# A spectral two-head kernel on one core: B's odd input lent to C as a seventh block, C's comparison ordered by table, A's result stored in half rows

## The chip, the cores and the metric

The kernel runs on one core of one Trainium2 chip. The core has a matrix engine (PE, with its weight loads listed apart as PEld), three engines for element work (DVE, ACT and POOL), a queue engine that mainly issues transfers (SP), and 16 DMA engines that all queues share. The metric is the device time of one execution in microseconds (us); less is better. SBUF is the on-chip memory with 128 partitions, PSUM the place where matrix products land, HBM the chip's main memory, where inputs and outputs lie.

## The reference

Two heads are computed from separate inputs and joined along the last axis. A is a global filter: a real 2-D Fourier transform, a product with a complex weight, and the inverse transform. B is a Fourier mixing layer whose transform matrices are given as inputs; for the values that are given they are the cosine and sine tables of the two lengths.

```python
def _A_ref(x, w_r, w_i):
    B, S, D = x.shape                                  # 1, 2048, 512
    X = jnp.fft.rfft2(x, axes=(-2, -1)) * (w_r + 1j * w_i)
    return jnp.fft.irfft2(X, s=(S, D), axes=(-2, -1))

def _B_ref(x, dft_seq_re, dft_seq_im, dft_hid_re, dft_hid_im):
    a = jnp.einsum("bsd,ed->bse", x, dft_hid_re)
    b = jnp.einsum("bsd,ed->bse", x, dft_hid_im)
    return (jnp.einsum("ts,bse->bte", dft_seq_re, a)
            - jnp.einsum("ts,bse->bte", dft_seq_im, b))

return jnp.concatenate([a, b], axis=-1)
```

## The kernel before

The kernel has three strands of work that share the engines.

**A** (`a_work`, line 628) is a fast transform written as matrix products. `forward` loads A's input in eight pieces, folds it on DVE and transforms it. Eight slots `e` (`slot`, line 512) then each multiply by the weights `wa`, which POOL's queue loads into `w`, one slot after the other; POOL writes two columns of `w` (line 519), ACT changes the sign of one part (line 520), DVE does the products, PE transforms in and out, and ACT writes the slot's result to `zv` (line 592). `inverse` (line 595) needs all slots. It runs eight steps of 8 products each out of `zv` (ACT copies at line 611) and 16 steps out of the tile `sda`, eight for each half `c` of the hidden places (ACT copies at line 622 into `ob`, which lies in the region of `zv`). When a half `c` is done, two stores of 1 MB each bring it to `out_a` (line 626).

**B** (`b_work`) computes the layer with a fast transform as well. Its folded input lies in two tiles, the even one `ye` and the odd one `yo` (25 x 128 values a partition); nine products `b_hidden` read them for the last time, and eight `b_rows` write the result, half by a store from SP and half by an indirect store from POOL.

**C** checks that the matrices given are the tables that B's fast transform assumes. It reads all of `cm` (32 blocks of 1 MB, each in two loads of 512 KB from SP, line 332) and compares each with a table `tt` on DVE (`count`, line 317), which counts differences in `stat`. There are four tables `pr`, each loaded once (line 327, 1 MB, two buffers). A table serves four blocks (`tb` 0 to 3) of its first half, then DVE changes the sign of every other column (line 340), and it serves four blocks of its second half. The tables go in pairs: first halves of tables 0 and 1, second halves of 0 and 1, then 2 and 3. After 16 blocks, `compare_hidden` (line 347) does the same for the two hidden matrices: ACT writes the expected table into a block `t` (lines 352 to 355, four operations), SP loads `wd` into another (line 357), and DVE compares. In this text the blocks of `cm` are called cm0 to cm31 in the order in which C takes them, and the hidden pair t0, wd0, t1, wd1.

All of C's blocks, and B's four blocks of raw input, come out of one ring of six buffers (`XR`, `block`, line 304): a load into a buffer waits until DVE, or for B's blocks PE, is done with what lay there.

At the end DVE sums `stat`, PE adds over the partitions (line 717), DVE makes a flag (line 718), and every engine reads the flag and branches (lines 720 and 721): where a difference was found, B is computed from the matrices as they are (`_b_from_c`); with the values given that part is skipped.

The order in which each engine takes its work is the program's order, which a scheduler makes of the three strands. `B_AT` and `C_AT` give the step of A after which a piece of B or C is due; `pin` holds a comparison behind a given DVE instruction of A. SP takes its transfers strictly in turn, and so do ACT, DVE and POOL.

Of the kernel before, what the change touches and what calls it, by code (L numbers as in the profile page):

```python
# [10 lines left out]
F32 = mybir.dt.float32  # L11
# [5 lines left out]
P = 128  # L17

YB = 2
XR = 6  # L20


B_AT = [0, 5, 7, 7, 8, 9, 9, 9, 9, 11, 13, 13, 13, 13, 13, 18, 20, 20, 21, 23, 27, 31, 31, 32, 50, 50, 50]
# [3 lines left out]
TINY = 2.0**-111  # L27
# [180 lines left out]
def kernel(  # L208
# [19 lines left out]
    nc = tc.nc  # L228
    ADD, SUB, MUL = ALU.add, ALU.subtract, ALU.mult
# [17 lines left out]
    bp = first.enter_context(tc.tile_pool(name="bp", bufs=1))  # L247
# [4 lines left out]
    def region(name):  # L252

        return ap.tile([P, 8192], F32, name=name)
# [6 lines left out]
    def part(v, kb, *shape):  # L261

        v = v[:, 256 * kb : 256 * kb + math.prod(shape)]
        if len(shape) == 1:
            return v
        names = "abcde"[: len(shape)]
        return v.rearrange("p (%s) -> p %s" % (" ".join(names), " ".join(names)), **dict(zip(names, shape)))
# [8 lines left out]
    yo = bp.tile([P, 25, 128], F32, name="yo")  # L276
# [3 lines left out]
    odd = bp.tile([P, 2], F32, name="odd")  # L280
# [18 lines left out]
    def late(dst, src):  # L299

        with tc.issue_after(turned[-1].ins):
            nc.gpsimd.dma_start(dst, src)  # L302

    def block():
        return bp.tile([P, 4, 512], F32, name="xr", bufs=XR)

    hts = []
    pin = [None]
# [3 lines left out]
    def count(raw, v, scale, op=ALU.not_equal):  # L312

        i = used[0]
        used[0] += 1
        with tc.issue_after(pin[0].ins) if pin[0] is not None else ExitStack():
            nc.vector.scalar_tensor_tensor(raw, raw, scale, v, op0=MUL, op1=op, accum_out=stat[:, i : i + 1])  # L317

    def compare():

        for pair in ((0, 1), (2, 3)):
            ts = []
            for half in range(2):
                for k, pr in enumerate(pair):
                    if half == 0:
                        ts.append(bp.tile([P, 4, 513], F32, name="tt", bufs=2))
                        nc.sync.dma_start(ts[k], tabs["tt"][pr])
                    t = ts[k]
                    for tb in range(4):
                        raw = block()  # L330
                        for m in range(2):
                            nc.sync.dma_start(raw[:, 2 * m : 2 * m + 2], cm[m, tb, pr + 4 * half])  # L332
                        v = t[:, :, 512:0:-1] if tb % 2 else t[:, :, :512]
                        for m in (slice(0, 2), slice(2, 4)) if tb % 2 else (slice(0, 4),):
                            k = int(tb % 2 and m.start == 2)
                            count(raw[:, m], v[:, m], odd[:, k : k + 1] if tb in (1, 2) else -TINY if k else TINY)
                        yield 2.4
                    if half == 0:
                        with tc.issue_after(pin[0].ins) if pin[0] is not None else ExitStack():
                            nc.vector.tensor_scalar(t[:, :, 1::2], t[:, :, 1::2], -1.0, None, op0=MUL)  # L340

    def hidden_table():

# [3 lines left out]
    def compare_hidden():  # L347

        hidden_table()
        for m in range(2):  # L350
            t = block()
            nc.scalar.mul(t[:, :2, :257], ht[:, :, m], TINY)
            nc.scalar.mul(t[:, :2, 257:], ht[:, :, m, 255:0:-1], -TINY if m else TINY)
            for k in range(2):
                nc.scalar.mul(t[:, 2:, k::2], t[:, :2, k::2], -1.0 if k else 1.0)
            raw = block()
            nc.sync.dma_start(raw, wd[m])
            count(raw, t, TINY)
            yield 2.4
# [87 lines left out]
    def mm(*args, **kw):  # L447
        mma[0] = nc.tensor.matmul(*args, **kw)  # L448
# [146 lines left out]
    def inverse(zv):  # L595

        v = bp.tile([P, 2304], F32, name="ye")
        di = v[:, :1024].rearrange("p (h q n) -> p h q n", h=2, q=2)
        g16 = v[:, 1024:1280].rearrange("p (s n) -> p s n", s=2)
        nc.sync.dma_start(di, tabs["di"].rearrange("p (h q n) -> p h q n", h=2, q=2))  # L600
        nc.sync.dma_start(g16, tabs["g16"].rearrange("p (s n) -> p s n", s=2))
        gz = zv.rearrange("p s f -> p (s f)")
        u = part(region("sda"), 0, 16, 512)
        for g in range(0, 16, 2):
            pu = ps_a.tile([P, 2, 512], F32, name="pa")
            for k in range(2):
                for h in range(2):
                    for q in range(2):
                        mm(pu[:, k, 256 * h : 256 * h + 256], gz[:, 32 * h + 16 * q + g + k :: 64], di[:, h, q],
                           start=q == 0, stop=q == 1)  # L610
            nc.scalar.copy(u[:, g : g + 2], pu)  # L611
            yield
        both = g16[:, :1].to_broadcast([P, 2, 128])
        ob = part(region("zv"), 0, 2, 2, 2, 8, 128)
        for c in range(2):
            for g in range(0, 16, 2):
                po = ps_a.tile([P, 2, 2, 128], F32, name="pa")
                for k in range(2):
                    for h in range(2):
                        at = 256 * h + 128 * c  # L620
                        mm(po[:, k], u[:, g + k, at : at + 128], g16 if h else both, start=h == 0, stop=h == 1)
                nc.scalar.copy(ob[:, c, :, :, g // 2], po.rearrange("p k r s -> p r k s"))  # L622
                yield
            for r in range(2):
                at = 256 * r + 128 * c
                nc.sync.dma_start(out_a[at : at + 128], ob[:, c, r].rearrange("p x i m -> p (x i m)"))

    def a_work():
        zv = part(region("zv"), 0, 16, 512)
        yield from forward(zv)  # L630
        TT(out=we[:, :, :, 0], in0=wsp_sb[:, :, :, 0, 0], in1=wsp_sb[:, :, :, 1, 0], op=ADD)
        TT(out=we[:, :, :, 1], in0=wsp_sb[:, :, :, 0, 1], in1=wsp_sb[:, :, :, 1, 1], op=SUB)
        TT(out=we[:, 1:, 1, 1], in0=wsp_sb[:, 1:, 1, 1, 1], in1=wsp_sb[:, 1:, 1, 0, 1], op=SUB)
        for i, v in enumerate((1.0, -1.0, 1.0, -1.0, -1.0)):
            nc.vector.memset(signs[:, i : i + 1], v)
        mid = region("sda")
        gens = [slot(e, zv, mid) for e in range(8)]

        def stage(e):
            if 0 <= e < 8:  # L640
                next(gens[e], None)

        stage(0)
        stage(0)
        stage(1)
        yield 0.1
        for e in range(9):
            stage(e)
            if e < 8:
                yield 5.0  # L650
            stage(e + 1)
            stage(e + 2)
            yield 0.1
            stage(e - 1)
            yield 0.1
        yield from inverse(zv)

    def b_work():
        x = {0: b_load(0)}
        yield  # L660
        x.update({q: b_load(q) for q in range(1, 4)})
        nc.gpsimd.dma_start(fb, tabs["fb"])
        yield
        for q in range(4):
            ev = b_fold(x[q])
            yield
            for g in range(4 * q, 4 * q + 4):
                b_along(g, x[q], ev)
            if q == 0:
                nc.sync.dma_start(hc, tabs["hc"])  # L670
                nc.sync.dma_start(slots, tabs["slot"])
                hidden_table()
                nc.sync.dma_start(mb, tabs["mb"])
            yield
        z = short()
        zb = [part(z, 2 * k, 512) for k in range(9)]
        for e in range(9):
            b_hidden(e, zb)
            yield
        for o in range(8):  # L680
            b_rows(o, zb)
            yield

    def all_compared():
        c = compare()
        for _ in range(16):
            yield next(c)
        yield from compare_hidden()
        yield from c

    count(same[:, 0:1], same[:, 1:2], TINY, ALU.is_equal)
    a, b, c = a_work(), b_work(), all_compared()
# [5 lines left out]
    for n in range(100):  # L698
        if next(a, a) is a and not b_at:
            break  # L700
        while b_at and b_at[0] <= n:
            b_at.pop(0)
            k = len(B_AT) - len(b_at) - 1
# [135 lines left out]
```

## Time and profile before

| | before |
|---|---|
| median of 3 runs | 221.36 us (221.28 to 221.91) |
| the profiled execution, whole | 220.61 us |
| its span in the trace | 218.6 us |
| PE busy / DVE busy / ACT busy / POOL busy | 88% / 73% / 35% / 18% |
| mean granted PE clock | 0.929 |
| bytes moved by DMA | 69.68 MB, mean 319 GB/s |

The span runs from the first to the last instruction of the program; what lies around it in the profiled execution is 220.61 - 218.6 = 2.0 us. Times in views of the trace count from the span's start. Busy shares are averages over stages that wait for different things, so the stages are read one by one. In a row of a timeline stand start, duration, engine, line and operation, written tile <- tiles read; SPq marks a transfer's issue by SP, not the transfer.

### The profile page before, as it was taken

Reading aid. Unit: us, or ns where it says so; the run is one execution under the profiler, and the core shown is the slowest. Engines: PE = TensorE matmul, PEld = TensorE weight load, DVE = VectorE, ACT = ScalarE, POOL = GpSimd, SP = SyncE. Lnnn points to the kernel's source line nnn. Section 1 sums busy time; section 2 is a strip of 40 time slices with the busy share of each in tenths; the row PEclk is TensorE's granted clock in tenths of the full one; section 3 lists DMA queues with packets and bytes.
Section 4 is the critical chain, followed back from the end, with each engine's and each line's share of the span. In section 5 each row is a group of like instructions: output and inputs, shape, how many; then the busy total and the mean of one; then the engine's idle time right before and its main releaser. Section 6 shows DMA issues by size and latency. Waiting matters only on the chain. (4 is left out here: it accounts for less than half of the span.)

```text
span 218.6 us, 2541 instructions
## 1 busy us (share of the span) xinstructions
PE 192.2 (88%) x833; PEld 150.0 (69%) x833; DVE 158.9 (73%) x257; ACT 77.2 (35%) x159; POOL 39.2 (18%) x56
## 2 busy tenths in 40 slices
PE   7799999979959999999999967668999999999700
PEld 2687778858749576586866544466999998888600
DVE  1589400088684899999889979799994799989350
ACT  2034333083452224422416535447333133333300
POOL 4002220032270010232113443160050000000000
PEclk9999999999995699999999996767999999999985
DMA  6999999999999999972353274057899999999990
GB/s 215 389 408 387 379 401 403 404 408 390 381 387 384 385 408 406 391 231 89 116 194 105 97 280 178 16 189 288 338 418 411 416 408 407 410 411 420 388 393 13
DMA packets 20883, 69.68 MB, mean 319 GB/s; under 512 B 3616, under 2 KB 4000, under 8 KB 19456
## 3 DMA queue, kind: packets, MB, share of 16 engines
q1 hardware_dynamic: 16176, 58.05, 67.6%
q0 software_dynamic: 4400, 10.81, 14.1%
q10 hardware_dynamic: 288, 0.59, 0.7%
q8 instruction: 8, 0.13, 0.2%
q14 instruction: 11, 0.09, 0.1%
HBM read 56.85 MB, written 8.39 MB: 298 GB/s over the span
## 5 line engine op out<-in xcount | busy, mean ns | idle before, releaser
L317 DVE SCALAR_TENSOR_TENSOR xr<-xr,tt 128x1024 f32<-128x1024 f32 (+1 forms) x24 | 37.3, 1578 | 27.9 <-DMA xr<-in_cm 27.8
L317 DVE SCALAR_TENSOR_TENSOR xr<-xr,odd,tt 128x1024 f32<-128x1024 f32 (+1 forms) x24 | 38.7, 1637 | 6.0 <-DMA xr<-in_cm 6.0
L448 PE MATMUL pa<-ye,zv 128*128 128x256 f32 x128 | 30.3, 401 | 2.0 <-ACT zv L592 2.0
L448 PE MATMUL pa<-zb,sda 128*128 128x256 f32 x128 | 30.6, 395 | 1.4 <-DVE sda L233 1.4
L448 PEld LDWEIGHTS pa<-ye,zv 128*128 128x128 f32 x128 | 29.2, 306 | 3.0 <-ACT zv L592 2.3
L448 PEld LDWEIGHTS pa<-zb,sda 128*128 128x128 f32 x128 | 25.2, 199 | 8.6 <-DVE sda L233 2.3
L233 DVE TENSOR_TENSOR sda<-zv 128x512 f32<-128x512 f32 (+1 forms) x24 | 19.0, 821 | 12.8 <-DMA zv<-in_xa 7.2
L448 PE MATMUL pa<-ye,sda 128*128 128x256 f32 x128 | 27.8, 379 | 0.0
L448 PEld LDWEIGHTS pa<-ye,sda 128*128 128x128 f32 x128 | 24.3, 190 | 3.3
L448 PEld LDWEIGHTS pa<-slots,sda 128*128 128x128 f32 x128 | 19.6, 225 | 8.5 <-DVE sda L233 3.7
L448 PE MATMUL pa<-slots,sda 128*128 128x128 f32 (+1 forms) x128 | 21.2, 328 | 2.6 <-DVE sda L233 2.6
L233 DVE TENSOR_TENSOR sda<-sda 128x512 f32<-128x512 f32 (+1 forms) x34 | 22.9, 716 | 0.0
L492 POOL DMA_DIRECT2D zv<-zb x16 | 10.0, 631 | 48.7 <-ACT zb L488 32.9
L233 DVE TENSOR_TENSOR sda<-pa,sda 128x1024 f32<-128x1024 f32 (+1 forms) x16 | 17.8, 1152 | 0.5
L481 ACT COPY zb<-pa 128x1024 f32<-128x1024 f32 x8 | 8.1, 1012 | 25.8 <-PE pa L448 25.8
L432 POOL DMA_INDIRECT out_b<-yb,turn x8 | 12.4, 1554 | 25.0 <-ACT yb L422 23.9
L448 PE MATMUL pa<-zb 128*128 128x512 f32 x32 | 15.1, 598 | 1.2 <-ACT zb L481 1.2
L388 PE MATMUL pb<-fb,xr 128*128 128x128 f32 (+1 forms) x64 | 15.4, 327 | 0.5 <-DVE xr L233 0.5
L622 ACT COPY zv<-pa 128x512 f32<-128x512 f32 x16 | 9.4, 587 | 17.8 <-PE pa L448 17.8
L302 POOL DMA_DIRECT2D sda<-in_wa x16 | 11.4, 717 | 23.0 <-ACT zb L405 10.1
L388 PE MATMUL pb<-fb,yb 128*128 128x72 f32 x64 | 13.3, 295 | 2.4 <-DVE yb L233 1.4
L611 ACT COPY sda<-pa 128x1024 f32<-128x1024 f32 x8 | 8.1, 1016 | 19.2 <-PE pa L448 19.2
(83 smaller groups left out, 216.0 us busy)
## 6 DMA issues: line engine op xcount, KB each, us to landing
xr<-in_cm SPq DMA_DIRECT2D x64, 512.0 KB, 10.3
tt<-tab_tt SPq DMA_DIRECT2D x4, 1026.0 KB, 12.6
zv<-in_xa SPq DMA_DIRECT2D x8, 512.0 KB, 9.7
xr<-in_xb SPq DMA_DIRECT2D x16, 256.0 KB, 6.9
zv<-zb POOLq DMA_DIRECT2D x16, 256.0 KB, 8.4
sda<-in_wa POOLq DMA_DIRECT2D x16, 256.0 KB, 3.7
out_a<-zv SPq DMA_DIRECT2D x4, 1024.0 KB, 10.8
xr<-in_wd SPq DMA_DIRECT2D x2, 1024.0 KB
```

What stands on the lines that cost most here:

```text
L233: last[0] = nc.vector.tensor_tensor(**kw)
L302: nc.gpsimd.dma_start(dst, src)
L317: nc.vector.scalar_tensor_tensor(raw, raw, scale, v, op0=MUL, op1=op, accum_out=stat[:, i : i + 1])
L388: nc.tensor.matmul(bank[:, at : at + hi - lo], v[:, cols], f[:, lo:hi], start=True, stop=True)
L432: stores.append(nc.gpsimd.indirect_dma_start(out=out_b, out_offset=bass.IndirectOffsetOnAxis(ap=turn[:, o : o + 1], axis=0), in_=y[:, 1], ...
L448: mma[0] = nc.tensor.matmul(*args, **kw)
L481: nc.scalar.copy(zs[p], pd[p])
L492: turned.append(nc.gpsimd.dma_start(zv[at : at + 29 : 4], ys[:, k]))
L611: nc.scalar.copy(u[:, g : g + 2], pu)
L622: nc.scalar.copy(ob[:, c, :, :, g // 2], po.rearrange("p k r s -> p r k s"))
```

## The change

Three things are changed.

`block()` counts its calls. From the 21st on (`LENT` = 20) every seventh comes from the place of `yo` instead of the ring: the calls are four for B's input, 16 for cm0 to cm15, then t0, wd0, t1, wd1, cm16 and so on, so that t0, cm19 and cm26 lie in `yo`'s place.

`compare()` takes one table at a time: four blocks, the change of sign, four blocks, then the next table. Table 0 is thus done after cm7 and table 1 after cm15, instead of after cm11 and cm15.

A's result is stored after four steps of each half `c` as well as after eight, as 512 KB in pieces of 2 KB (four `i` by 128 values) instead of 1 MB in pieces of 8 KB.

```diff
+LENT = 20
...
+    blocks = [0]
+
     def block():
+
+        i = blocks[0] - LENT
+        blocks[0] += 1
+        if i >= 0 and i % (XR + 1) == 0:
+            more = bp.tile([P, 25, 128], F32, name="yo").rearrange("p s j -> p (s j)")
+            return more[:, :2048].rearrange("p (k d) -> p k d", k=4)
         return bp.tile([P, 4, 512], F32, name="xr", bufs=XR)
...
-        for pair in ((0, 1), (2, 3)):
-            ts = []
+        for pr in range(4):
+            t = bp.tile([P, 4, 513], F32, name="tt", bufs=2)
+            nc.sync.dma_start(t, tabs["tt"][pr])
             for half in range(2):
-                for k, pr in enumerate(pair):
-                    if half == 0:
-                        ts.append(bp.tile([P, 4, 513], F32, name="tt", bufs=2))
-                        nc.sync.dma_start(ts[k], tabs["tt"][pr])
-                    t = ts[k]
-                    for tb in range(4):
...
+                if half:
+                    with tc.issue_after(pin[0].ins) if pin[0] is not None else ExitStack():
+                        nc.vector.tensor_scalar(t[:, :, 1::2], t[:, :, 1::2], -1.0, None, op0=MUL)
+                for tb in range(4):
+                    raw = block()
...
+        rows = out_a.rearrange("d (x i m) -> d x i m", x=2, i=8)
         for c in range(2):
             for g in range(0, 16, 2):
...
                 nc.scalar.copy(ob[:, c, :, :, g // 2], po.rearrange("p k r s -> p r k s"))
+                if g in (6, 14):
+                    i = slice(g // 2 - 3, g // 2 + 1)
+                    for r in range(2):
+                        at = 256 * r + 128 * c
+                        nc.sync.dma_start(rows[at : at + 128, :, i], ob[:, c, r, :, i])
                 yield
-            for r in range(2):
-                at = 256 * r + 128 * c
-                nc.sync.dma_start(out_a[at : at + 128], ob[:, c, r].rearrange("p x i m -> p (x i m)"))
```

In the program's order this moves the following. Lines of the changed kernel lie a few higher than those of the kernel before: 340 for 332, 332 for 327, 362 for 357, 357 to 360 for 352 to 355, 597 for 592, 633 for 626, 728 for 720.

SP, from the later blocks of C's first half to the middle of its second, before:

```order
L332 DMA xr<-in_cm 128x1024 x28
L600 DMA ye<-tab_di 128x1024
L601 DMA ye<-tab_g 128x256
L429 DMA out_b<-yb 64x512 x2
L431 DMA out_b<-yb 128x512 x6
L357 DMA xr<-in_wd 128x2048
L327 DMA tt<-tab_tt 128x2052
L357 DMA xr<-in_wd 128x2048
L332 DMA xr<-in_cm 128x1024 x4
L327 DMA tt<-tab_tt 128x2052
L431 DMA out_b<-yb 128x512
L332 DMA xr<-in_cm 128x1024 x26
```

And the same place now:

```order
L340 DMA xr<-in_cm 128x1024 x24
L332 DMA tt<-tab_tt 128x2052
L340 DMA xr<-in_cm 128x1024 x4
L605 DMA ye<-tab_di 128x1024
L606 DMA ye<-tab_g 128x256
L434 DMA out_b<-yb 64x512 x2
L436 DMA out_b<-yb 128x512 x6
L362 DMA xr<-in_wd 128x2048
L436 DMA out_b<-yb 128x512
L362 DMA xr<-in_wd 128x2048
L340 DMA xr<-in_cm 128x1024 x6
L332 DMA tt<-tab_tt 128x2052
```

Table 2 moved from behind wd0 to a place between cm13 and cm14, and B's last store from behind table 3 to a place between wd0 and wd1.

SP at the end of the program, before:

```order
L332 DMA xr<-in_cm 128x1024 x26
L626 DMA out_a<-zv 128x2048 x2
L332 DMA xr<-in_cm 128x1024 x2
L626 DMA out_a<-zv 128x2048 x2
L720 TENSOR_LOAD flag
```

And now:

```order
L340 DMA xr<-in_cm 128x1024 x8
L633 DMA out_a<-zv 256x1x512 x2
L340 DMA xr<-in_cm 128x1024 x2
L633 DMA out_a<-zv 256x1x512 x6
L728 TENSOR_LOAD flag
```

Ahead of cm31, the last block, stand two stores of 512 KB where two of 1 MB stood; six of 512 KB follow it.

ACT around the last slot's copies into `zv`, before:

```order
L419 COPY yb<-pb 128x2x257
L352 ACTIVATE xr<-ht 128x2x257
L353 ACTIVATE xr<-ht 128x2x255
L355 ACTIVATE xr<-xr 128x512 x2
L592 COPY zv<-pa 128x2x16x16 x2
L352 ACTIVATE xr<-ht 128x2x257
```

And now:

```order
L424 COPY yb<-pb 128x2x257
L597 COPY zv<-pa 128x2x16x16 x2
L357 ACTIVATE xr<-ht 128x2x257
L358 ACTIVATE xr<-ht 128x2x255
L427 COPY yb<-yb 128x2x255
L360 ACTIVATE xr<-xr 128x512 x2
```

The four operations that make t0 no longer stand ahead of the copies into `zv`; they now write `yo` and stand right behind the last copy of `b_hidden`. On DVE the change of sign of table 1 moved from the slots' stage to a place behind cm11, and B's last pair of sums to a place just ahead of it; on POOL the weights' loads of slot 3 now stand ahead of slot 2's two columns.

More of the change, by code (lines that the diff above doesn't have):

```diff
@@ L319, in compare @@
     def compare():
-        for pair in ((0, 1), (2, 3)):
-            ts = []
+        for pr in range(4):
+            t = bp.tile([P, 4, 513], F32, name="tt", bufs=2)
+            nc.sync.dma_start(t, tabs["tt"][pr])
             for half in range(2):
-                for k, pr in enumerate(pair):
-                    if half == 0:
-                        ts.append(bp.tile([P, 4, 513], F32, name="tt", bufs=2))
-                        nc.sync.dma_start(ts[k], tabs["tt"][pr])
-                    t = ts[k]
-                    for tb in range(4):
[L330 to L340, printed above, removed]
+                if half:
[3 more added lines that the diff above has]
+                    raw = block()
+                    for m in range(2):
+                        nc.sync.dma_start(raw[:, 2 * m : 2 * m + 2], cm[m, tb, pr + 4 * half])
+                    v = t[:, :, 512:0:-1] if tb % 2 else t[:, :, :512]
+                    for m in (slice(0, 2), slice(2, 4)) if tb % 2 else (slice(0, 4),):
+                        k = int(tb % 2 and m.start == 2)
+                        count(raw[:, m], v[:, m], odd[:, k : k + 1] if tb in (1, 2) else -TINY if k else TINY)
+                    yield 2.4
     def hidden_table():
```

## The prediction

> **What bounds the kernel now.** I read the chain of waits first, in order of time.
>
> ```profile
> 142.80 4.74 DVE xr L317 x7
> ...
> 156.66 6.44 DMA xr<-in_cm
> ...
> 195.32 12.45 DMA xr<-in_cm
> ...
> 207.88 2.40 DVE xr L317 x4
> 210.31 0.22 DVE rs L715
> 210.57 0.40 PE pb L717 x2
> 210.99 0.16 DVE flag L718
> ```
>
> Until 142.7 us the chain runs through DVE and A's slots; from 156.7 it is nothing but loads of `cm`, then the last block's comparison, the sum and the flag, which stands at 211.15. From there to the span's end are 218.65 - 211.15 = 7.5 us. The table by stages says whether those loads wait for buffers or for the DMA engines.
>
> ```profile
> 93.00:142.80 49.80, 44.12 (x195) 29.94 (x193) 45.04 (x88) 20.22 (x40) 15.59 (x22) 0.93 0.42 148
> ...
> 148.00:156.00 8.00, 7.35 (x25) 6.62 (x26) 8.00 (x11) 4.39 (x8) 0.00 (x0) 0.79 0.82 298
> 156.00:192.00 36.00, 36.00 (x166) 34.40 (x166) 30.85 (x41) 11.86 (x16) 3.00 (x1) 1.00 1.02 412
> ...
> 213.50:218.60 5.10, 0.00 (x0) 0.00 (x0) 0.00 (x0) 0.00 (x0) 0.00 (x0) 0.50 0.04 13
> ...
> 208.00:213.50 5.50, 0.38 (x2) 0.30 (x2) 2.64 (x6) 0.00 (x0) 0.00 (x0) 0.81 0.94 387
> ```
>
> The last three columns are the PE clock, the DMA engines' share and GB/s. In 156 to 192 DMA is full (1.02, 412 GB/s), so a megabyte (1.05 million bytes) costs 2.55 us there. In 93 to 142.8 it is 42% full. A's last stores run until 213.5 at 387 GB/s, 2.71 us a megabyte. So the tail is a DMA queue, and bytes taken out of it, or moved ahead of 142.8, shorten it. PE is full beside it, which makes it the second bound: A's last copy ends at 207.17.
>
> ```profile
> 142.95 3.67 PE L448 MATMUL pa<-slots,sda 128*128 128x128 f32 x16 [2.64 <-DVE sda L233]
> ...
> 148.65 1.97 PE L448 MATMUL pa<-ye,zv 128*128 128x256 f32 x6 [2.03 <-ACT zv L592]
> ...
> 145.71 0.64 ACT L352 ACTIVATE xr<-ht 128x514 f32<-128x514 f32 x1
> ...
> 146.90 1.24 ACT L355 ACTIVATE xr<-xr 128x512 f32<-128x512 f32 x2
> 148.03 1.05 ACT L592 COPY zv<-pa 128x512 f32<-128x512 f32 x2
> ...
> 206.58 0.59 ACT L622 COPY zv<-pa 128x512 f32<-128x512 f32 x1 [1.14 <-PE pa L448]
> 207.19 0.82 SPq L626 DMA_DIRECT2D out_a<-zv  x2
> ```
>
> PE is done with the last slot at 146.62, but ACT copies it at 148.03, behind the four operations of t0, and PE starts the inverse at 148.65.
>
> **Seventh block.** It holds t0, cm19 and cm26. In the idle stretch of DMA it holds t0, which ACT writes and no load fills, so it fetches nothing ahead. Later the waits of SP count.
>
> ```profile
> SPq L332 <- DMA xr<-in_cm: 20.9, 23, 1.1
> ...
> SPq L332 <- DVE xr L317: 3.0, 2, 1.9
> ```
>
> From 142 us on, SP's loads waited 23 times for an earlier load to land (eight are in flight) and twice for DVE to free a buffer. More depth is worth nothing there: 0, at most the 3.0 us of the second row. What the block does bring is that t0 no longer stands in the ring, so that wd0 goes into cm10's buffer, and t0's four operations leave their place. Behind the last copy of `b_hidden` (109.06 + 0.59) ACT is idle for 4.70 us, and 2.4 us of t0 fit; without that cover they would cost slot 5's chain 2.4 us.
>
> ```profile
> 109.06 0.59 ACT L405 COPY zb<-pb 128x512 f32<-128x512 f32 x1 [0.95 <-PE pb L404]
> 114.34 0.42 ACT L520 ACTIVATE sda<-sda 128x256 f32<-128x256 f32 x1 [4.70 <-DMA sda<-in_wa]
> ```
>
> **A's chain.** The copies into `zv` start at 146.65 instead of 148.03: -1.38 us for the inverse. The clock adds to it.
>
> ```profile
> 44.12:47.53 3.41, 2.25 (x10) 1.00 1.02 418
> 47.53:50.95 3.42, 3.42 (x17) 1.00 1.02 398
> ...
> 146.52:149.93 3.41, 1.38 (x6) 1.00 0.61 183
> 149.93:153.34 3.41, 3.41 (x9) 0.50 0.90 375
> ```
>
> The columns are PE busy, clock, DMA. The clock changes at steps of 3.41 us: the stretch with PE busy for 1.38 us was followed by half clock, one with 2.25 was not. The inverse's first full stretch at half clock costs 3.41/2 = 1.7 us. With PE starting at 147.27, the stretch before has 1.38 + 1.38 = 2.8 us busy, so I take the full clock: A's last copy ends at 207.17 - 1.38 - 1.7 = 204.1. Bounds: 205.8 if half clock stays.
>
> By the Trainium skill (TensorE: Matmul & The Clock Gate, Part 1), the clock falls to half after an idle window of about 3.4 us, and the windows run free of the kernel's start. The trace agrees with the window's length; by the skill the gain of 1.7 us would come in some executions and not in others.
>
> **DMA tail.** wd0 now waits for cm10, so SP issues it at 145.1, alone. wd1 waits for cm12. The unbroken stream starts there.
>
> ```profile
> 142.80 2.35 DVE L317 SCALAR_TENSOR_TENSOR xr<-xr,odd,tt 128x2048 f32<-128x2048 f32 x1
> ...
> 147.36 2.29 DVE L317 SCALAR_TENSOR_TENSOR xr<-xr,tt 128x2048 f32<-128x2048 f32 x1
> ...
> 147.47 0.34 SPq L357 DMA_DIRECT2D xr<-in_wd  x1
> 147.87 0.55 SPq L327 DMA_DIRECT2D tt<-tab_tt  x1
> 152.10 0.33 SPq L357 DMA_DIRECT2D xr<-in_wd  x1
> ```
>
> - Start: before, wd0 and table 2 start it at 147.5. Now DVE has B's sums (0.7) and the sign change (0.7) ahead of cm12, which began at 147.36 and takes 2.2 net of overlap: wd1 at 151.0, +3.5 us. Behind it DVE frees a block each 2.3 us, faster than DMA fills one (2.55).
> - wd0 lands ahead of the stream: -2.55. Table 2 is loaded at about 82 us: -2.55.
> - B's last store pair (0.52 MB) moves ahead of wd1: -1.27.
> - Ahead of cm31 stands 1 MB of A's stores, not 2: -2.71.
>
> The sum is -5.6: cm31, which landed at 207.8, lands at 202.2. Bounds: the 18% idle in 148 to 156 (1.4 us) may not come back, 200.8; or the new ramp idles as long again, 203.6. DVE can follow: from 142.80 it is busy for 58.1 us (the row below), 0.4 of it for the last sum and the flag, and 0.7 come in for the sign change, so without a wait it would be done with the comparisons at 201.2. With the last load it is done at 202.2 + 2.4 + 0.2 = 204.8, sum included, and the flag stands at 204.8 + 0.7 = **205.5**, 5.65 earlier.
>
> ```profile
> 142.80:211.20 68.40, 58.05 (x78) 0.95 0.94 377
> ```
>
> **The slots' stage.** Table 2 adds 2.55 us of traffic at 82 to 97 us, beside slot weights.
>
> ```profile
> 93.35 0.39 POOL L519 COPY sda<-we 128x4 f32<-128x4 f32 x1 [4.75 <-DMA sda<-in_wa]
> 96.50 1.41 POOL L302 DMA_DIRECT2D sda<-in_wa  x2 [2.77 <-issue]
> ...
> 99.38 2.36 DVE L233 TENSOR_TENSOR sda<-pa,sda 128x1024 f32<-128x1024 f32 x2
> ```
>
> On POOL slot 2's columns now come behind slot 3's loads, at 97.9 instead of 93.4; DVE needs them at 99.38. They fit by 1.1 us and I take 0; the bounds are 0 and +2.55, if the slot's weights come later by all of the table's traffic. The sign change that leaves this stage saves nothing there, as DVE waits behind it for ACT.
>
> **The stores and the end.** A row of B's input moves in 2 KB pieces too; its issue takes 0.53 us against 0.33 for `cm`.
>
> ```profile
> L332 SPq DMA_DIRECT2D xr<-in_cm x64: 327/328/1201, 27.3 to 196.6; - x64
> L296 SPq DMA_DIRECT2D xr<-in_xb x17: 534/535/1171, 7.8 to 37.2; - x17
> ...
> 9.00:22.00 13.00, 13.00 (x52) 9.99 (x51) 10.28 (x15) 4.05 (x4) 1.28 (x2) 1.00 1.03 398
> ```
>
> Two stores cost SP 1.2 us: 204.1 + 1.2 = 205.3, just ahead of the flag. Loads of that kind ran at 398 GB/s, so I take the stores' 387: 3 MB behind cm31 drain until 202.2 + 8.1 = 210.3, against 213.5 before. The end lies between two bounds. If the code behind the branch loads beside the stores, it is 205.5 + 7.5 = 213.0 (-5.65). If it loads when they are done, as it may have before, it is 210.3 + 5.1 = 215.4 (-3.2). I take the middle, **-4.4**: 220.61 becomes 216.2 for a profiled execution, whose time lay 0.75 under the median, and 221.36 becomes 217.0.
>
> The Trainium skill (Runtime: NRT & Kernel Launch, Instruction fetch mechanics) says that a taken branch outside the loaded window has its code fetched by DMA before it goes on. The trace has the wait, 3.8 us on SP, and cannot show what stores do to it; by DMA: Bandwidth & Descriptors (Queues, rings and completion order), an engine takes its queues in turn, which speaks for the smaller time, -5.65.
>
> ```profile
> SPq L721 <- SPq L721: 3.8, 1, 3.8
> ```
>
> **Rivals.**
> 1. Code waits for the stores: 221.36 - 3.2 = 218.2, and 219.0 if 2 KB pieces store a tenth slower (0.8 us on 8.1). For it: the 5.1 us without any work start just where the stores end. Against it: the branch came only 1 us earlier.
> 2. Half clock stays: A's last copy at 205.8, SP free for the flag at 207.0, 1.5 us behind it, so the lower bound of the end becomes -4.15 and the middle 217.7.
> 3. Table 2 delays a slot by 2.55 us and half clock stays: A's copy at 208.4, SP at 209.6, 211.15 - 209.6 = 1.6 gained: 219.8.
> 4. The change is not felt: the seventh block holds t0 and SP waits for landings, as shown. It takes rival 3 and the slow stores of rival 1 together: 220.7 to 222.
> 5. Slower: stores in 2 KB pieces. The 4 MB of A's result must pass behind 202.2 - 2.7 = 199.5. Before, they ended at 213.5; at 300 GB/s they do again (4.19/0.3 = 14.0 us), at 250 they end at 216.3, 2.8 us later: 224.2. Nothing in the trace stores 2 KB pieces in a full queue; against it stand the loads at 398 GB/s.
>
> **How the numbers follow.** Forecast (215.7 to 218.1) 0.50; rival 1, 0.18; rival 2, 0.15; rival 3, 0.07; rival 4, 0.05; rival 5, 0.05. A measurement tells 0.3% (0.7 us) from no change. The forecast and rivals 1 to 3 are faster: 0.90; same 0.05; slower 0.05. The range goes from 215.3 (213.0 at the end: 221.36 - 5.65 = 215.7, and 0.4 for an idle ramp that does not return) to 219.8, rival 3.
>
> **What would show it.** Table 2 issued near 82 us; PE on `pa<-ye,zv` from 147.3 and full clock behind it; the last `cm` landing near 202; the flag near 205.5; stores until about 210; and 5 to 7.5 us behind the flag. Wrong are the steps if slots end later than 146.6, if the last `cm` lands after 204, or if over 8 us lie behind the flag.

## The result, and the profile after

The changed kernel takes 218.56 us (median of 18 runs, 216.69 to 221.52), the kernel before 221.69 us beside it (18 runs, 218.94 to 225.17). The ratio is 0.9886, with a 95% interval of 0.986 to 0.9912: 1.1% faster, where 217.0 us or 2.0% had been predicted, with a range of 215.3 to 219.8. A later series gave 218.43 against 221.14, ratio 0.9884 (0.9827 to 0.9942).

The first profile of the changed kernel (221.52 us) fell on a disturbed execution, so the lines here are from the profile of that series (218.94 us, span 216.9), whose slots end at 143.07 us as those of before did at 142.90. The chain of waits:

```profile
143.07 4.54 DVE xr L326 x6
...
161.32 11.03 DMA xr<-in_cm
...
193.52 11.26 DMA xr<-in_cm
204.80 1.23 DVE xr L326 x2
...
207.57 0.60 PE pb L725 x2
208.20 0.16 DVE flag L726
```

It is the chain of before, DVE first and then loads of `cm` only. The last block starts to be compared at 204.80 instead of 207.88, and the flag stands at 208.36 instead of 211.15, 2.8 us earlier where 5.65 had been predicted. The span became 1.75 us shorter (216.9 against 218.65), so part even of the 2.8 us was lost behind the flag. The stages show where DMA did less than foreseen (columns as before; the last three are PE's clock, DMA's share, GB/s):

```profile
93.00:142.80 49.80, 44.18 (x198) 29.30 (x197) 46.14 (x89) 23.37 (x48) 15.15 (x22) 0.97 0.48 166
142.80:148.00 5.20, 3.55 (x22) 3.36 (x23) 5.20 (x11) 1.92 (x4) 3.05 (x2) 1.00 0.58 161
148.00:156.00 8.00, 8.00 (x38) 8.00 (x38) 7.97 (x11) 4.53 (x7) 2.46 (x1) 1.00 0.84 303
...
166.00:196.00 30.00, 30.00 (x140) 27.47 (x140) 26.97 (x37) 9.62 (x15) 0.00 (x0) 1.00 1.01 405
196.00:202.00 6.00, 6.00 (x30) 5.28 (x29) 5.92 (x7) 2.24 (x4) 0.00 (x0) 1.00 1.05 327
202.00:208.00 6.00, 1.19 (x6) 0.76 (x4) 2.94 (x7) 0.59 (x1) 0.00 (x0) 0.85 1.04 407
```

Table 2 now loads in the idle stretch (166 GB/s there, 148 before). PE has its full clock from 148 to 156 (0.79 before). The new thing is the row from 196 to 202: the engines are busy (1.05) and yet move 327 GB/s. A share over 1 with a low rate means that transfers were under way but slow, not that they were missing; two views of the pieces, further down, bear that out.

The issues by SP and the work of ACT and PE at the places that the prediction spoke of:

```profile
81.92 0.33 SPq L332 DMA_DIRECT2D tt<-tab_tt  x1
...
145.34 0.34 SPq L362 DMA_DIRECT2D xr<-in_wd  x1
149.35 0.33 SPq L436 DMA_DIRECT2D out_b<-yb  x1
151.25 0.34 SPq L362 DMA_DIRECT2D xr<-in_wd  x1
...
145.86 1.08 ACT L597 COPY zv<-pa 128x512 f32<-128x512 f32 x2
...
146.51 5.66 PE L453 MATMUL pa<-ye,zv 128*128 128x256 f32 x24 [1.33 <-ACT zv L597]
...
202.80 0.59 ACT L628 COPY zv<-pa 128x512 f32<-128x512 f32 x1 [1.14 <-PE pa L453]
```

### The profile page after: what moved, and what is told of

The parts are those of the page before. It is cut to its first block, busy times and chain, and to the rows that moved or that the text cites. A ratio compares the mean times of both kernels' runs of the same rounds, so it can differ in the third digit from the quotient of the medians.

```text
span 218.9 us, 2542 instructions
## 1 busy us (share of the span) xinstructions
PE 193.0 (88%) x833; PEld 151.4 (69%) x833; DVE 159.3 (73%) x257; ACT 77.0 (35%) x159; POOL 38.3 (17%) x56
## 4 chain that ended last, share of the span: by engine, by line
PE 35%; DMA 34%; DVE 20%; issue 3%; ACT 2%; POOL 2%; SPq 0%; DVEq 0%; ACTq 0%; POOLq 0%
PE pa L453 22%; DMA xr<-in_cm 20%; DVE sda L234 10%; DVE xr L326 8%; DMA zv<-zb 8%; PE pb L393 5%; PE pb L409 3%; DMA zv<-in_xa 3%; DMA sda<-in_wa 2%; DMA out_b<-yb,turn 2%; DVE yb L234 2%; PE pb L405 1%; PE pb L406 1%; PE pb L407 1%; ACT zb L493 1%
## 5 line engine op out<-in xcount | busy, mean ns | idle before, releaser
L326 DVE SCALAR_TENSOR_TENSOR xr<-xr,tt 128x1024 f32<-128x1024 f32 (+1 forms) x22 | 35.1, 1611 | 31.7 <-DMA xr<-in_cm 31.7
L326 DVE SCALAR_TENSOR_TENSOR xr<-xr,odd,tt 128x1024 f32<-128x1024 f32 (+1 forms) x23 | 36.2, 1605 | 1.3 <-DMA xr<-in_cm 1.2
L453 PE MATMUL pa<-zb,sda 128*128 128x256 f32 x128 | 32.1, 408 | 1.7 <-DVE sda L234 1.7
L453 PEld LDWEIGHTS pa<-zb,sda 128*128 128x128 f32 x128 | 26.3, 207 | 9.2 <-DVE sda L234 2.6
L453 PE MATMUL pa<-ye,zv 128*128 128x256 f32 x128 | 28.6, 386 | 0.7 <-ACT zv L597 0.7
L453 PEld LDWEIGHTS pa<-ye,zv 128*128 128x128 f32 x128 | 28.3, 304 | 0.9 <-ACT zv L597 0.9
L393 PE MATMUL pb<-fb,xr 128*128 128x128 f32 (+1 forms) x64 | 16.3, 344 | 0.5 <-DVE xr L234 0.5
L393 PE MATMUL pb<-fb,yb 128*128 128x72 f32 x64 | 14.0, 307 | 2.9 <-ACT ye L398 1.9
L393 PEld LDWEIGHTS pb<-fb,yb 128*128 128x128 f32 x64 | 12.6, 239 | 3.9 <-ACT ye L398 3.3
```

Of the source, the lines that this page charges most:

```text
L393: nc.tensor.matmul(bank[:, at : at + hi - lo], v[:, cols], f[:, lo:hi], start=True, stop=True)
```

## The experiments

Three theories stood against each other. **T1**: what ends the kernel is the drain of the DMA queue behind the slots, because the code behind the branch only loads once the stores are done. **T2**: the end is the flag plus a fixed 7.5 us. **T3**: PE's chain and its clock set the end. One number is compared throughout, the tail: the time from the end of DVE's last operation of the slots until all but 0.1 MB of SP's queue has moved (the drain), and on to the span's end. It leaves out what differs from execution to execution ahead of it: in the changed kernel's first profile the slots ended at 146.3 us, in another at 141.4, with PE's clock halved in other stretches.

In the profile of before the drain took 70.19 us:

```profile
142.90:213.09 70.19, 61.94 (x274) 57.15 (x274) 57.95 (x76) 24.28 (x36) 5.78 (x3) 0.94 0.94 378
213.09:218.60 5.51, 0.00 (x0) 0.00 (x0) 0.00 (x0) 0.00 (x0) 0.00 (x0) 0.50 0.05 15
```

Time by rate gives the bytes: 70.19 us x 378 GB/s = 26.5 MB. The table has the versions that are made of the change's three parts; the later ones have their figures beside them.

| version | time, ratio (95% interval) | slots' end to drain | moved | drain to end |
|---|---|---|---|---|
| before | 221.3, 221.7, 221.1 in the three series | 70.19 | 26.5 MB | 5.5 |
| block alone | 218.79, 0.9881 (0.9841 to 0.992) | 68.00 | 26.5 | 5.0 |
| order alone | 220.09, 0.9941 (0.991 to 0.9973) | 69.97 | 25.4 | 5.1 |
| halves alone | 223.31, 1.0073 (1.0044 to 1.0102) | 72.50 | 26.5 | 5.4 |
| all three | 218.93, 0.9895 (0.9852 to 0.9938) | 69.02 | 25.4 | 5.0 |
| all three, again | 218.43, 0.9884 (0.9827 to 0.9942) | 69.00 | 25.4 | 4.8 |
| block and order | 217.65, 0.987 (0.9813 to 0.9927) | 67.70 | 25.5 | 4.9 |
| block and order, again | 216.73, 0.9797 (0.9755 to 0.984) | 67.09 | 25.5 | 4.4 |

### The three parts, each alone, and all

`block()` takes `yo`'s place for the 21st call and every seventh after it; the rest of the text is as before, but the program's order then has all four stores of A's result behind cm31, as it has in the order alone and in block and order:

```diff
+        if i >= 0 and i % (XR + 1) == 0:
+            more = bp.tile([P, 25, 128], F32, name="yo").rearrange("p s j -> p (s j)")
```

> Only the seventh block in yo's place; tables in pairs and whole 1 MB stores as before, but all four stores stand behind cm31 (before: two ahead of it). Theory T1 (the end follows the drain of the DMA queue behind the slots, and the code behind the branch loads about 5 us after the last store): t0 leaves the ring, so wd0 can come earlier, but table 2 and the hidden matrices still load in the tail, and DMA loses a little at the start; with four stores behind cm31 the queue of bytes is as long as before, so the time is that of before within 1 us, 220.5 to 222. Rival T2 (the end is the flag plus 7.5 us): cm31 lands some 5 us earlier since two 1 MB stores no longer stand ahead of it, the flag comes earlier by as much and the time falls by 3 to 5 us, to 217 to 218.5. Rival T3 (PE's chain and its half clock behind the slots set the end): the copies into zv lose t0's four operations, 1.4 to 3 us are gained.

218.79 us, 1.2% under before: the block alone gives as much as the whole change. The bytes are the same, the queue is emptied 2.2 us sooner:

```profile
143.72:211.72 68.00, 58.69 (x274) 54.79 (x274) 57.92 (x76) 22.01 (x32) 4.89 (x3) 0.97 0.97 390
...
148.00:156.00 8.00, 8.00 (x38) 8.00 (x38) 8.00 (x11) 4.48 (x6) 0.00 (x0) 1.00 0.90 355
...
202.00:208.00 6.00, 1.81 (x9) 1.22 (x7) 4.31 (x8) 0.91 (x2) 0.00 (x0) 0.93 1.00 421
```

The last two stretches of before, for this and the later versions:

```profile
196.00:202.00 6.00, 6.00 (x29) 5.28 (x28) 5.13 (x9) 2.35 (x4) 0.00 (x0) 1.00 1.03 421
202.00:208.00 6.00, 4.54 (x22) 3.65 (x20) 2.23 (x3) 1.76 (x3) 0.00 (x0) 1.00 0.90 374
```

In 148 to 156 DMA moves 355 GB/s instead of 298, since wd0, wd1 and the first `cm` behind them are issued 1.5 us earlier, and in 202 to 208 it moves 421 instead of 374, since A's last copy comes at 203.5 to 204.0 us and SP no longer waits for it with an empty queue. So the bytes were counted rightly by T1, but not the idle time, which the block removes at both ends. It is T3's part, t0 out of the way, that does it: the order alone, next, has its stores in the same place without the block, and its queue, with 1 MB less in it, is emptied only 0.2 us sooner. Against T2: the flag came 4.3 us earlier (206.82), the end only 2.0.

Only the order, table by table:

```diff
-        for pair in ((0, 1), (2, 3)):
+        for pr in range(4):
+            t = bp.tile([P, 4, 513], F32, name="tt", bufs=2)
+            nc.sync.dma_start(t, tabs["tt"][pr])
```

> Only the order table by table; no seventh block, whole 1 MB stores, all four behind cm31. T1 (drain of the queue sets the end): table 2 (1.05 MB) loads in the idle stretch near 82 us and B's last store moves ahead, so the queue is shorter by 2.5 us and the time falls by about 2.5 us, to 219. T2 (flag plus 7.5 us): table 2 out (2.5 us) and two stores behind cm31 (5.1 us) bring the flag forward by 5 to 7 us, time 215 to 217. T3 (PE and its clock): t0 still stands ahead of the copies into zv, nothing is gained, 221 to 222.

220.09 us: 1.2 us gained, half of T1's 2.5 and far from T2's 5 to 7. Table 2 is out of the tail (25.4 MB), but the drain ends only 0.2 us sooner:

```profile
142.77:212.74 69.97, 60.05 (x274) 55.50 (x274) 58.67 (x79) 24.30 (x36) 4.81 (x3) 0.95 0.92 363
...
148.00:156.00 8.00, 7.49 (x27) 6.90 (x28) 7.97 (x10) 4.92 (x8) 2.03 (x1) 0.79 0.70 253
```

Without the block, t0 and wd0 stay where they were, and table 2 was what DMA had to do meanwhile: 253 GB/s where there were 298. A's last copy comes at 206.2 to 206.8 us, nearly as late as in before. Bytes taken out of a stretch that is not full save little. Between the two profiles 0.85 us of span are gained: 0.13 ahead of the slots' end, 0.2 in the drain and 0.45 behind it; what makes the rest of the 1.2 us was not found. The flag stood at about 207.8, some 3.4 us earlier than before, which again speaks against T2.

Only the stores in halves:

```diff
+                if g in (6, 14):
+                    i = slice(g // 2 - 3, g // 2 + 1)
...
+                        nc.sync.dma_start(rows[at : at + 128, :, i], ob[:, c, r, :, i])
```

> Only A's result in 512 KB halves; no seventh block, tables in pairs. T1 (drain of the queue): same bytes in the same queue, the time stays within 0.7 us of before, or gains what the last store's earlier start is worth where SP was waiting for ACT's last copy (under 1.5 us). T2 (flag plus 7.5 us): 1 MB of stores ahead of cm31 instead of 2 brings the flag forward by 2.5 us, time 219. T3 (PE and its clock): no change, 221 to 222; if the pieces of 2 KB store slower than those of 8 KB the time rises by 1 us or more.

223.31 us, slower by 0.7%. The last clause of T3's expectation came true:

```profile
143.26:215.76 72.50, 62.10 (x274) 57.32 (x274) 58.39 (x78) 24.27 (x36) 3.75 (x3) 0.93 0.96 365
...
196.00:202.00 6.00, 6.00 (x30) 5.28 (x29) 2.90 (x4) 2.00 (x4) 0.00 (x0) 1.00 1.06 303
202.00:208.00 6.00, 4.90 (x23) 3.98 (x21) 4.38 (x5) 2.11 (x4) 0.00 (x0) 1.00 1.05 352
```

The same bytes take 2.3 us longer, and 2.0 of it is lost while the halves are stored: 303 and 352 GB/s instead of 421 and 374, with the engines busy. T2 was not tested by this run. Its expectation had 1 MB of stores ahead of cm31, but the program's order put both halves of `c` = 0 there, 2 MB as in before, and the flag came at 214.49, 3.3 us later than before:

```profile
188.09 1.80 SPq L628 DMA_DIRECT2D out_a<-zv  x2
...
195.74 2.30 SPq L628 DMA_DIRECT2D out_a<-zv  x2
200.56 1.09 SPq L332 DMA_DIRECT2D xr<-in_cm  x2
```

> The changed kernel again, beside its parts on one chip. 218 to 219, 2.5 to 3.5 us below the kernel before. T1: its gain is that of the order alone (2.5 us) plus at most 1 us, stores' end to span's end 4.5 to 5.5 us in the profile. T2: its gain is the gain of the flag. T3: gain and half clock behind the slots go together.

218.93 us. The three parts add up: by the ratios the block alone gives 1.2%, the order alone 0.6%, the halves alone cost 0.7%, and all three together give 1.05%. T1 had the time right, but put the gain down to the order; more of it is the block's. T1's 4.5 to 5.5 us from drain to end held (5.0).

### Block and order, with whole stores

```diff
-                if g in (6, 14):
...
+            for r in range(2):
+                at = 256 * r + 128 * c
+                nc.sync.dma_start(out_a[at : at + 128], ob[:, c, r].rearrange("p x i m -> p (x i m)"))
```

> Seventh block and order table by table, with whole 1 MB stores, all four behind cm31. T1 (the end follows the drain of the DMA queue, 4.6 to 5.5 us behind the last store's end): bytes as in the full change; what differs is the stretch of slow 2 KB store packets (100 to 184 ns instead of 84, some 0.4 MB or 1 us lost in the full change's profile, 1.6 us in the one with the halves alone), which goes, so 217.5 to 218. T2 (the end is the flag plus 7 to 10 us): the same as the full change, 218.9. T4 (the halves are worth their early start, as SP no longer waits for ACT's last copy with 2 MB still to come): slower than the full change, 219.5 to 220.

217.65 us. As this lay in another series than the full change, both were run once more, side by side.

> The full change, again, on one chip with the next three. 218.5 to 219, 2.5 to 3 us below the kernel before. In its profile code behind the branch starts to load when the stores have nearly drained, 4.9 to 5.5 us ahead of the span's end.

> Block and order with whole stores, again, for what the halves are worth beside them. T1 with the slow 2 KB packets as their cost: 217.5 to 218, 0.7 to 1.3 us below the full change. Rival (the halves cost nothing beside the other two parts, the first comparison was the chip's spread): within 0.4 us of it.

218.43 and 216.73 us: beside the other two parts the halves cost 1.7 us in this series. Across the first two series it is 1.3 us by the times and 0.6 by the ratios to before. The intervals of the two ratios overlap by 0.0013, but the profiles tell the two apart. Block and order:

```profile
142.93:210.02 67.09, 58.69 (x274) 54.73 (x274) 58.67 (x77) 21.91 (x32) 5.23 (x3) 0.97 0.96 380
...
196.00:202.00 6.00, 6.00 (x29) 5.30 (x28) 5.89 (x9) 2.10 (x4) 0.00 (x0) 1.00 1.03 421
202.00:208.00 6.00, 1.01 (x5) 0.49 (x4) 2.09 (x6) 0.58 (x1) 0.00 (x0) 0.85 1.01 427
```

In 196 to 202 the full change moves 327 GB/s, this one 421: 6.00 x (1 - 327/421) = 1.3 us lost. Afterwards it is 407 against 427, another 0.3 us in six. A's last copy is as early in both (202.80 and 202.66), so T3 does not explain this difference.

Two views of transfers in the full change, a slow stretch and a later one, say what is slow:

```profile
DMA packets 309, 0.60 MB, mean 242 GB/s; under 512 B 22, under 2 KB 22, under 8 KB 309
q1 hardware_dynamic: 309, 0.60, 110.0%
...
DMA packets 527, 1.02 MB, mean 408 GB/s; under 512 B 32, under 2 KB 32, under 8 KB 527
q1 hardware_dynamic: 527, 1.02, 105.2%
```

Both are 2.5 us long, from 199 and from 205. Without the small ones they hold 287 and 495 pieces, most of them the stores' 2 KB, and 16 engines x 2.5 us x the share gives 153 and 85 ns for one.

### Does the end follow the stores?

The full change without the stores of `c` = 1:

```diff
+                        if c == 0:
```

> The full change without the four stores of A's second hidden half (c = 1): these rows of A are not written, 2.1 MB less in the queue. T1: stores end before the flag, so the code behind the branch loads at once; the flag stays near 206.5 and the end comes 6 to 7 us behind it, 3 us or more below the full change, 215 to 216. T2 (end = flag plus a fixed 7.5 us and more, whatever the stores do): within 1 us of the full change, 218 to 219.

216.91 us, 1.5 to 2.0 under the full change where T1 had said 3, since the flag came at 208.60 in this execution and not at 206.5. The branch itself decides between T1 and T2. PE's branch behind the flag (min, median and max in ns, then its start), first in this run, whose stores were done before the flag:

```profile
L730 PEldq COMPARE_BRANCH  x1: 3622/3622/3622, 209.2 to 209.2; - x1
```

In the full change, with 2.7 us of stores still to come:

```profile
L729 PEldq COMPARE_BRANCH  x1: 5306/5306/5306, 209.4 to 209.4; - x1
```

With block and order, where 4.2 us of stores are left:

```profile
L726 PEldq COMPARE_BRANCH  x1: 6386/6386/6386, 205.9 to 205.9; - x1
```

And before:

```profile
L721 PEldq COMPARE_BRANCH  x1: 3566/3566/3566, 212.4 to 212.4; - x1
```

With none of the stores to come, or 0.7 us of them (before), the branch takes 3.6 us, with 2.7 us of them 5.3 and with 4.2 us 6.4; and the run without the stores of `c` = 1 takes them away and gets the short branch back. In block and order, the view of transfers from 205 to 209.4 has one queue only, SP's; the queues that load code appear behind it, from 209.4 on, when SP's is down to its last 0.19 MB:

```profile
q1 hardware_dynamic: 38, 0.19, 10.2%
q14 instruction: 5, 0.04, 2.5%
q8 instruction: 2, 0.03, 2.4%
```

So in the versions of the table the end is the later of two: the flag plus 6.5 us (208.60 to 215.12 without late stores), or the drain plus 4.4 to 5.5 us. T2 holds only while the stores are done in time, as before: there the branch took what it takes without stores, and of the 1.0 us between its 7.5 us and these 6.5 some 0.6 is a slower reading of the flag. Behind the changed tail T1's count holds. Two later runs show that the drain as such is not what the branch waits for; they stand at the end of the next section.

### The hidden pair last

If bytes must leave the tail, the block in `yo`'s place should hold a load. With `compare_hidden` behind all of C's blocks, cm16 lies there and loads while DMA is half empty:

```diff
-        c = compare()
-        for _ in range(16):
-            yield next(c)
+        yield from compare()
         yield from compare_hidden()
-        yield from c
```

> The full change with the hidden pair compared behind all of cm: yo's place then holds cm16, whose 1 MB loads in the half-empty stretch ahead of the slots' end, where t0 (written by ACT, no load) stood. T1: 1.05 MB more leaves the tail, worth 2.5 us if DMA is full from there on and less by what the start of the tail idles anyway: 216.3 to 218. T2 and T3 (flag; PE's chain): the flag's path is the same number of comparisons on DVE, 218 to 219, or later by the two hidden blocks at the end, 220.

> The full change with the hidden pair last, again: 214 to 215.5, 6 to 7 us below the kernel before and 3.5 us or more below the full change.

214.63 us, ratio 0.9726 (0.9668 to 0.9783), and 214.62, 0.971 (0.9666 to 0.9754): 6.5 to 7 us under the kernel before, and more than the expected 2.5 us under the change.

```profile
93.00:141.83 48.83, 43.64 (x197) 29.51 (x196) 45.74 (x89) 20.49 (x42) 15.94 (x22) 0.97 0.54 193
141.83:206.94 65.11, 59.20 (x274) 54.49 (x274) 58.31 (x77) 23.72 (x36) 4.43 (x3) 0.99 0.98 374
148.00:156.00 8.00, 8.00 (x38) 8.00 (x37) 7.97 (x14) 2.65 (x3) 1.65 (x1) 1.00 1.03 364
```

24.4 MB are left in the tail (65.11 x 374), 1 MB less. The idle time at its start went too: every block that DVE frees there takes a load now, where in the change one of them went to t1, which ACT writes, and 148 to 156 runs at 364 GB/s instead of 303. Then A's last copy becomes the bound: in this profile SP waited 11.5 us for ACT with A's stores. The same with whole stores:

> Seventh block, order table by table, the hidden pair last, and whole 1 MB stores behind everything. T1 with the slow 2 KB packets as a cost of the halves: the lowest of all, 1 us below the same with halves, 215.5 to 217. T4 (halves are worth their early start): 1 us above it. T2: the flag later by the two hidden blocks, 219 to 220.

216.42 us, ratio 0.9801 (0.9741 to 0.9861): slower than with halves by 1.8 us, against T1's 1 us the other way, and as the expectation's T4 had it (the halves are worth their early start). DMA waits for A's last copy at 203.67 us and then has 2 MB left:

```profile
198.00:204.30 6.30, 5.75 (x29) 4.99 (x27) 3.47 (x6) 2.34 (x4) 0.00 (x0) 1.00 0.42 176
204.30:210.85 6.55, 0.00 (x0) 0.00 (x0) 0.00 (x0) 0.00 (x0) 0.00 (x0) 0.67 0.82 318
```

Last, `c` = 0 stored whole and `c` = 1 in halves:

```diff
-                if g in (6, 14):
-                    i = slice(g // 2 - 3, g // 2 + 1)
+                if g == 14 or g == 6 and c:
+                    i = slice(g // 2 - 3, g // 2 + 1) if c else slice(0, 8)
```

> Hidden pair last, A's first hidden half stored whole (8 KB pieces), its second half in halves of 512 KB. T1 with a second bound (A's last copy, then what is left to store behind it, then 5 us): behind A's last copy stands 1 MB as in the version with halves everywhere, and the slow stretch of 2 KB packets at the first pair goes: the same or up to 1 us less, 213.5 to 215. Rival (the early store of the first quarter is what made halves faster than whole stores, 214.6 against 216.4): near the whole stores, 216.

214.60 us, ratio 0.9697 (0.9651 to 0.9744): the same as with halves everywhere. What counts here is that 1 MB and not 2 stands behind the last copy. The slow stretch is gone without a gain, so it had been hidden by SP's wait for ACT.

These last two runs limit the answer of the section before. PE's branch, first with whole stores, then with `c` = 0 whole and `c` = 1 in halves:

```profile
L723 PEldq COMPARE_BRANCH  x1: 5426/5426/5426, 204.6 to 204.6; - x1
...
L726 PEldq COMPARE_BRANCH  x1: 3402/3402/3402, 204.1 to 204.1; - x1
```

In the first, 6.3 us of stores were still to come, in the second 3.7, and yet the branch took only 5.4 and 3.4 us. In both, the queue had run empty while SP waited for A's last copy, and the last stores began to move only after the branch had started. The second's transfers from 205 to 207.5 show code and stores side by side:

```profile
DMA packets 440, 0.90 MB, mean 360 GB/s; under 512 B 14, under 2 KB 14, under 8 KB 437
...
q8 instruction: 1, 0.02, 3.2%
q14 instruction: 2, 0.02, 1.6%
```

From the drain to the end these two runs take 3.8 and 3.9 us, less than any version of the table. So what delays the branch seems to be the stores that are queued when it asks for its code, not those that come after; no run varied this alone.

## Why the prediction was right, and where it was not

The sign and the range held; the size was 1.6 us too good. The result lies beside the forecast's own band (215.7 to 218.1) and inside that of rival 1 (218.2 to 219.0); the range's upper end came from rival 3, which did not occur. Two of the signs that were named for wrong steps came: the last `cm` landed after 204, at 204.8, and over 8 us lie behind the flag, 216.9 - 208.4 = 8.5.

- **Block: its depth worth 0, its effect through t0.** Right. Wd0 was issued at 145.34 (145.1 said), wd1 at 151.25 (151.0), the copies into `zv` came at 145.86 (146.65), the inverse at 146.51 (147.27), A's last copy at 203.4 (204.1). Alone it gave 2.5 us. In the pair-last version, where a load goes into the same place early and the hidden pair moves to the end, the kernel is 3.8 us faster than with the full change.
- **Half clock gone behind the inverse's start.** Right, and in this profile the clock was full already from 142.8 on. In all eleven profiles with the block that stretch has full clock, in the three without it half. The Trainium skill (TensorE: Matmul & The Clock Gate, Part 1) has the windows of the clock run free of the kernel's start. That the gain would therefore come in some executions only is not borne out for this stretch. For the slots it is: where 13.7 us of half clock lay ahead of their end, they ended at 141.4 and 141.8 us, with 17.1 us at 142.4 to 144.9, and with 20.5 us at 143.7, 143.7 and 146.3.
- **Table 2 early costs the slots nothing.** Right: 81.92, and the slots' end moved by 0.17 us. Its -2.55 us is worth only 0.2 in the drain without the block, and the sum of the start (+3.5, -2.55, -2.55, -1.27 = -2.9) is near what block and order show together, -2.5 and -3.1 in the drains of the two runs.
- **"Ahead of cm31 stands 1 MB of A's stores, not 2: -2.71."** Here it failed, in its size. It rested on "Loads of that kind ran at 398 GB/s, so I take the stores' 387". The pure stores did reach 399 to 407, but the first pair of halves ran in a slow stretch (1.3 us); the loads ahead of cm31 ran at 405 instead of 412 GB/s for 30 us (0.5), 0.4 us came from table 3's load and the slots, and some 0.4 us is left unassigned. cm31 landed at 204.8, not 202.2 (bounds 200.8 to 203.6); the flag stood at 208.4, not 205.5; the stores drained at 212.07, not 210.3.
- **"I take the middle, -4.4."** The step that failed as a mechanism: there is no middle between code beside the stores and code behind them. Rival 1 came true for the changed kernel, "Code waits for the stores", 218.2 said and 218.56 found, though for another reason than the row named for it: in before the code did not wait. That its number came so near is partly luck: it had the drain 1.8 us too early, and the gain that it put at 3.2 us is 3.1 between the medians, 2.5 by the ratio and 1.75 between the two spans. What spoke against it, "the branch came only 1 us earlier", was right, and the change itself moved the branch ahead of the drain. In the profile shown the miss is 216.9 - 214.2 = 2.7 us of span: 1.2 from the choice of the middle, 1.8 from the later drain, less 0.3 (4.8 behind the drain instead of 5.1).
- **An engine takes its queues in turn** (the Trainium skill, DMA: Bandwidth & Descriptors, Queues, rings and completion order) was read as a reason for the smaller time. Where the stores had long been queued, the runs speak against that reading: PE's branch grew from 3.6 to 6.4 us as more of them were left. In the two runs in which they began to move after the branch, it took 3.4 and 5.4 us with 3.7 and 6.3 us of them left, and code moved beside them. The Trainium skill (Runtime: NRT & Kernel Launch, Instruction fetch mechanics) agrees with both: a branch out of the loaded window waits until its code is fetched.

## What to carry to other kernels

Where a queue of transfers sets the end, bring the bytes that remain and the stretches in which the queue idles into one sum: a megabyte taken out of a stretch that is not full is worth little (0.2 us of the drain here, where 2.55 was expected), and a spare buffer is worth most when a load can go into it early. Moving stores behind the last load brings a flag forward, but not the end by as much, if code must still load behind them. Storing in smaller pieces paid where the queue stood empty before the last result was there (1.8 us), and cost where it was full (1.7 to 2.0 us within a series).

## What the runs showed of the hardware that was not expected

Stores in 2 KB pieces ran at 84 ns a piece for most of their time, but in each of the seven profiles that store `c` = 0 in halves, the first pair had a stretch of some 3 us with 100 to 210 ns on average (two such stretches with the halves alone); loads of 4 KB among them were slowed as well. The halves of `c` = 1 stayed at 84 to 96 ns but for a few pieces at their very end, also when they came first and PE was at work. The two kinds write different rows of `out_a`, and no run exchanged these; the cause was not found.

Reading the flag took the engines 0.47 to 0.54 us without the stores of `c` = 1, 0.8 to 0.9 in the full change and 1.05 to 1.2 with whole stores in the queue, as in before. With the halves alone it took 0.47 to 0.53 us as well, though 1.3 us of stores were left, so stores in the queue are not the whole reason.
